# Two interleaved attention layers: normalised rows shared with GpSimd, more PSUM places, a new order, fewer waits

## The chip, the core and the metric

The kernel runs on one core of a Trainium2 chip. A core has five engines with queues of their own: TensorE (PE, matmuls into PSUM), VectorE (DVE), ScalarE (ACT), GpSimd (POOL) and SyncE (SP, which issues transfers). PSUM, into which TensorE writes, has eight banks of 512 f32 per partition. The metric is the device time of one execution in microseconds; lower is better.

## The reference

Two blocks, A and B, are each applied twice to x of 2048 rows and 512 columns, 32 heads of 16:

```
x = x + A(layernorm(x)); x = x + B(layernorm(x))      # twice

A: for each of 4 segments of 512 rows:
   a_dot = softmax(q k^T * scale + causal mask) v
   a_mem = phi(q) M / (phi(q) z + 1e-6)               # phi(t) = t+1 if t > 0 else exp(t)
   o = g * a_mem + (1 - g) * a_dot
   M += phi(k)^T v;  z += sum(phi(k))
B: phi_q = [softmax(q w), softmax(-q w)], phi_k alike  # per head
   o = phi_q (phi_k^T v) / (phi_q sum(phi_k) + 1e-6)
each followed by a product with wo
```

## The kernel before

The program first builds a list of 3416 operations (`Program.add`), each with its engine or a choice of engines, its inputs and outputs as tiles, and a planner's cost. Nothing is planned when it runs: four tables written out in the file fix everything. `ORDER` lists the operations in the order in which the queues are filled; a number of 10000 and more is a score operation whose matmuls are interleaved with those of the one before it, and a negative number is a group of idle matmuls on a tile of zeros (L1431), which keep TensorE's clock up. `ENGINE` has one letter for each operation that has a choice of engines. `SLOTS` has a digit for each tile: which buffer, or which PSUM place of its kind, it gets. `AFTER` is a list of 126 pairs (x, y). `replay` reads the tables, and `finalize` turns each operation's needs into semaphore waits.

A pair (x, y) of `AFTER` makes operation x wait for operation y, though y is no input of x (`ops[x].need.add(y)` at the end of `replay`). In all 126 x stands on GpSimd and y on VectorE.

The rows are handled in tiles of 128. For each segment of 512 rows and each layer, the work is:

- `ln` (L790 on): per row tile the statistics (`stats`, L801; `aggr`, L802), the reciprocal deviation (`veps` and `pow`, L811 and L813, mostly on GpSimd; L807 and L808 on ScalarE), and the normalised rows `xn` (L817, VectorE, two tiles a buffer). A transposing transfer from SP's queue then makes xnT (tiles xA, xB or EQ) of them; at the start and at the turn between the layers TensorE transposes instead (L601).
- `a_proj`: q, k and v for block A; the copies out of PSUM (`k.copy`, `q.copy`, `v.copy`, all by the helper at L579) are on ScalarE or VectorE by `ENGINE`; small rearrangements `lo` (L907) and `kp` (L938) on VectorE, ScalarE or GpSimd; `phik`, `phiq` on ScalarE and VectorE.
- `a_att`: 288 score operations (`score`, 36 for each segment and layer), each filling a pair of PSUM banks, each followed by one exponential of 128 x 1024 on ScalarE (`exp`, L1104, into a tile PT). On the diagonal tiles follow two masks: `mask.odd` (L1110, tile D, VectorE or GpSimd) and `mask.even` (L1113, in place in PT, GpSimd). Then the products with v (`pv`), their division (`r1` and `norm`, L1138 and L1139), the memory's part (`amadd`, L1149), the output product and the addition to X (L1165; or through TensorE with `resid.act` at L579).
- `b_keys`, `b_queries`, `b_out`: block B, whose exponentials are at L1200 and L1285, sums at L1207 (GpSimd) and L1209, `bk.z` at L1220 to L1222 (ScalarE, VectorE or GpSimd), `bq.wide` at L1304 (ScalarE or GpSimd), divisions at L1342.

All matmuls but the idle ones and the transposes have line L520. The kinds of PSUM places are in `self.PS.kinds`: "st" a pair of banks for a score operation; "gen" and "pv" one bank for a single result; "two" and "wide" are those of block B's output and of the turn and the tail.

Blocks A and B, and the segments, are woven into each other by `ORDER`. Each engine works its queue strictly in that order.

Of the kernel before, what the change touches and what calls it, by code (L numbers as in the profile page):

```python
# [275 lines left out]
class Program:  # L276
# [22 lines left out]
    def R(self, *key):  # L299
        r = self.fixed.get(key)  # L300
        if r is None:
            r = self.fixed[key] = Res()
        return r
# [49 lines left out]
    def replay(self):  # L353
# [34 lines left out]
        for x, y in AFTER:  # L388
            ops[x].need.add(y)
# [1086 lines left out]
```

## Time and profile before

| | |
|---|---|
| median of 3 runs | 478.36 us (478.14 to 478.48) |
| the profiled execution | 478.63 us, of which its span 476.9 us |
| granted TensorE clock | 1.00 over the span |
| transfers | 35.86 MB in 115091 packets, mean 75 GB/s |

A group in the profile reads: line, engine, operation, out<-in by tile names, shapes, count | busy us, mean ns of one | idle time of the engine before them, and what ended most of it. A wait reads: who waited <- for whom: total us, times, longest. A row of the time line reads: start, length, engine, line, operation. PE is TensorE's matmuls, PEld its weight loads, which run ahead beside them. Times in rows are us from the span's start.

The kernel has a lead-in of some 13 us (loads, first statistics), two layers of four segments, a turn between the layers near 200 to 240 us, and a tail from about 440 us.

### The profile page before, as it was taken

The numbers are of one execution on the slowest core, as the hardware profiler recorded it, in microseconds if no ns is written. First come the engines' busy times: TensorE is split into PE (matmuls) and PEld (weight loads), VectorE is DVE, ScalarE is ACT, GpSimd is POOL, SyncE is SP. The second block draws the span as 40 slices with busy tenths as digits, with TensorE's granted clock in tenths as the row PEclk, the third lists the DMA queues.
The fourth block names the chain that finished last, engine by engine and source line by source line (L and its number), as shares of the span: only waits on it lengthen the run. The fifth ranks groups of instructions, "written<-read, shape, count | busy, mean of one in ns | idle before, by whom it ended". The sixth has DMA issues, their size and how long they took to land.

```text
span 476.9 us, 19206 instructions
## 1 busy us (share of the span) xinstructions
PE 465.2 (98%) x8309; PEld 319.3 (67%) x8309; DVE 424.0 (89%) x1008; ACT 429.7 (90%) x666; POOL 268.9 (56%) x435
## 2 busy tenths in 40 slices
PE   7999999999999999999999999999999999999997
PEld 6786677567756567557687666766765666665763
DVE  6999899989998988688999999999998888978885
ACT  3989999999999999986799899989999999999742
POOL 3686758656756685510267575784677578761100
DMA  8679661342422132320346417155434121313366
GB/s 264 115 202 147 144 92 25 69 69 47 48 46 47 25 65 51 36 55 4 67 62 97 74 21 134 25 75 83 59 63 63 25 47 33 51 38 58 70 128 186
DMA packets 115091, 35.86 MB, mean 75 GB/s; under 512 B 106816, under 2 KB 115008, under 8 KB 115008
## 3 DMA queue, kind: packets, MB, share of 16 engines
q1 hardware_dynamic: 112608, 32.54, 38.3%
q10 hardware_dynamic: 2400, 2.11, 1.4%
q8 instruction: 65, 1.06, 0.9%
q14 instruction: 18, 0.15, 0.1%
HBM read 6.32 MB, written 2.10 MB: 18 GB/s over the span
## 4 chain that ended last, share of the span: by engine, by line
PE 59%; DVE 18%; ACT 17%; DMA 3%; POOL 2%; issue 1%; POOLq 0%; DVEq 0%
PE PS L520 57%; ACT PT L1104 12%; DVE D L1110 2%; DVE stats L801 2%; DVE Vt L1228 2%; ACT Ek L1200 2%; DVE xn L817 1%; PE PS L601 1%; DMA EQ<-xn 1%; PE PS L1431 1%; DMA OT<-O 1%; DVE O L1139 1%; ACT K L1285 1%; DVE X L1165 1%; DVE Zk L1209 1%
## 5 line engine op out<-in xcount | busy, mean ns | idle before, releaser
L1104 ACT ACTIVATE PT<-PS 128x1024 bf16<-128x1024 f32 x288 | 284.6, 1083 | 7.8 <-PE PS L520 7.5
L1110 POOL TENSOR_TENSOR D<-PT,modd 128x256 bf16<-128x256 bf16 x133 | 91.6, 699 | 54.2 <-ACT PT L1104 39.1
L1113 POOL TENSOR_SCALAR_AFFINE_SELECT PT<-PT 128x512 bf16<-128x512 bf16 x128 | 83.9, 664 | 30.8 <-DVE D L1110 27.4
L520 PEld LDWEIGHTS PS<-VT,PT 128*128 128x128 bf16 x2048 | 75.0, 96 | 19.2 <-POOL PT L1113 2.5
L520 PE MATMUL PS<-VT,PT 128*128 128x17 bf16 x2048 | 82.4, 171 | 0.7 <-POOL PT L1113 0.2
L520 PE MATMUL PS<-QT,K 32*128 32x64 bf16 (+2 forms) x2176 | 77.9, 213 | 0.3
L520 PE MATMUL PS<-VT,D 128*128 128x17 bf16 x512 | 59.9, 170 | 0.0
L520 PEld LDWEIGHTS PS<-QT,K 32*128 32x128 bf16 x2176 | 41.5, 93 | 20.6 <-ACT PT L1104 10.5
L1110 DVE TENSOR_TENSOR D<-PT,modd 128x256 bf16<-128x256 bf16 x123 | 42.9, 362 | 2.9 <-ACT PT L1104 1.5
L520 PEld LDWEIGHTS PS<-VT,D 128*128 128x128 bf16 x512 | 43.2, 96 | 0.0
L1228 DVE TENSOR_TENSOR Vt<-PS,Zk 128x1024 bf16<-128x1024 f32 (+1 forms) x34 | 39.0, 1158 | 2.0 <-PE PS L520 1.0
L801 DVE BATCH_NORM_STATS2 stats<-X 128x6 f32<-128x512 bf16 x56 | 37.3, 681 | 2.5 <-DMA X<-in_A_x_dram 2.2
L1200 ACT ACTIVATE Ek<-PS 128x512 bf16<-128x512 f32 x64 | 37.6, 664 | 0.9 <-PE PS L520 0.9
L520 PE MATMUL PS<-WA_v,xA 128*128 128x256 bf16 x256 | 36.6, 273 | 0.1
L520 PE MATMUL PS<-WA_k,xA 128*128 128x256 bf16 x256 | 36.3, 273 | 0.2 <-POOL xA L907 0.2
L520 PE MATMUL PS<-xA,WA_q 128*128 128x128 bf16 x512 | 35.7, 219 | 0.5 <-DVE MS L986 0.2
L1165 DVE TENSOR_TENSOR X<-X,PS 128x512 bf16<-128x512 bf16 x50 | 33.7, 679 | 2.2 <-PE PS L520 1.8
L1207 POOL TENSOR_TENSOR Vt<-Ek 128x512 f32<-128x512 bf16 x24 | 27.9, 1164 | 12.9 <-ACT Ek L1200 10.4
L520 PEld LDWEIGHTS PS<-xA,WA_q 128*128 128x128 bf16 x512 | 29.8, 98 | 4.6 <-issue 0.6
L520 PE MATMUL PS<-WA_o,OT 128*128 128x512 bf16 x128 | 32.0, 380 | 0.6 <-DMA OT<-O 0.4
L520 PE MATMUL PS<-WB_o,OT 128*128 128x512 bf16 x128 | 32.1, 379 | 0.1
L1304 POOL COPY O<-rho 128x512 bf16<-128x512 bf16 x24 | 14.9, 634 | 26.5 <-DVE rho L1297 23.3
(157 smaller groups left out, 980.7 us busy)
## 6 DMA issues: line engine op xcount, KB each, us to landing
X<-in_A_x_dram SPq DMA_DIRECT2D x3, 512.0 KB, 9.9
EQ<-in_B_wqkv_dram SPq DMA_DIRECT2D x2, 512.0 KB, 5.4
out_dram<-X SPq DMA_DIRECT2D x8, 128.0 KB, 2.0
out_dram<-X ACTq DMA_DIRECT2D x8, 128.0 KB, 1.9
OT<-O SPq DMA_TRANSPOSE x42, 3.2
WB_v<-in_B_wqkv_dram SPq DMA_DIRECT2D x1, 512.0 KB, 4.3
WA_o<-in_A_wo_dram SPq DMA_DIRECT2D x1, 512.0 KB, 6.5
WB_o<-in_B_wo_dram SPq DMA_DIRECT2D x1, 512.0 KB, 4.7
```

The source lines that it names most:

```text
L520: return e.matmul(o, l, r, start=st, stop=sp, tile_position=(basep(l), basep(o)))
L601: ins = e.transpose(self.bank(gen).bitcast(BF16)[:, dt * 128:(dt + 1) * 128], src()[:, dt * 128:(dt + 1) * 128], self.ident[:])
L801: self.dve(lambda e, t=t, src=src: e.bn_stats(self.stats[:, t, :], src()), 0.603, [held() if held else R("X", t)], [R("stats", t)], name=" ...
L817: self.dve(lambda e, t=t, n=n, xn=xn: e.tensor_scalar(xn.ap[:, n], self.X[:, t, :], self.mv[:, t, 0:1], self.rstd[:, t:t + 1], op0=ALU.sub ...
L1104: self.act(lambda e, st=st, pt=pt: e.activation(pt.ap[:].rearrange("p b c -> p (b c)"), self.ps[:, st.slot[0] * 512:st.slot[0] * 512 + 102 ...
L1110: self.either(lambda e, d=d, k=k, pt=pt: e.tensor_tensor(d.ap[:, :, k, :].rearrange("p b (z c) -> p b z c", z=2), self.ends(pt.ap[:, :, 25 ...
L1113: self.pool(lambda e, q=quarters: e.affine_select(q(), q(), [[0, 4], [1, 128]], ALU.is_ge, 0.0, base=0, channel_multiplier=-1), 0.6, [pt() ...
L1165: self.dve(lambda e: e.tensor_tensor(X[:, t, :], X[:, t, :], self.bank(gen), ALU.add), 0.6, [R("X", t), gen()], [R("X", t)], name="resid")
L1200: self.act(lambda e, sgn=sgn, Ek=Ek, gen=gen: e.activation(Ek.ap[:, sgn, :], self.bank(gen), ACT.Exp, scale=1.0 - 2.0 * sgn), 512, [gen()] ...
L1207: self.pool(lambda e, Ek=Ek, sums=sums: e.tensor_tensor(sums(), *(Ek.ap[:].rearrange("p s (h j) -> p s h j", h=H)[:, :, :, 8 * k:8 * k + 8 ...
L1228: self.dve(lambda e, w=w, n=n, Vt=Vt, Zk=Zk, gen2=gen2: e.tensor_tensor(self.signed(Vt)[:, w, :, 0:16], self.bank(gen2).rearrange("p (h d) ...
L1304: P.add(("act", "pool"), {"act": lambda e, dst=dst, src=src: e.activation(dst(), src(), ACT.Copy), "pool": lambda e, dst=dst, src=src: e.t ...
```

## The change

Four things are changed at once.

1. In `ln` the operation `xn` may be on VectorE or on GpSimd (`either` in place of `dve`), the same instruction on either. The new `ENGINE` puts 27 of 64 on GpSimd, 11 in the first layer and 16 in the second.
2. "st" gets the pair of banks 6 and 7; "gen" gets banks 3 and 2.
3. `AFTER` and the two lines of `replay` that read it go: 126 waits of GpSimd for VectorE.
4. `ORDER`, `ENGINE` and `SLOTS` are new. The operations are the same 3416. Idle matmuls are 143 in place of 129, and 75 score operations are interleaved with the one before in place of 67. Of the operations with a choice of engines these change sides (before, then after):

| operation | ScalarE | VectorE | GpSimd |
|---|---|---|---|
| xn | - | 64, 37 | 0, 27 |
| k.copy | 18, 13 | 10, 15 | - |
| v.copy | 17, 16 | 15, 16 | - |
| bk.z | 4, 9 | 7, 6 | 21, 17 |
| bq.wide | 8, 6 | - | 24, 26 |
| resid.act | 12, 10 | 2, 4 | - |
| xnT.copy | 6, 4 | 6, 8 | - |
| boT.copy | 5, 6 | 3, 2 | - |
| fold.copy | 1, 2 | 7, 6 | - |
| kp | 2, 3 | 13, 15 | 17, 14 |
| lo | 6, 6 | 11, 10 | 15, 16 |
| mask.odd | - | 123, 126 | 133, 130 |

```diff
 ORDER = (
...
-AFTER = (
-    (389, 128), (164, 47), (181, 51), (353, 38), (371, 144), (201, 191), (212, 152), (202, 192), (213, 175), (1142, 370), (260, 43), (261, 154),
...
 ENGINE = (
...
 SLOTS = (
...
                 last.mate = op
                 last.need.update(op.need)
             last = op
-        for x, y in AFTER:
-            ops[x].need.add(y)
...
         self.PS.kinds = {
-            "st": [(0, 1), (2, 3), (4, 5)],
+            "st": [(0, 1), (2, 3), (4, 5), (6, 7)],
             "pv": [(7,), (6,), (5,), (4,)],
-            "gen": [(7,), (6,), (5,), (4,)],
+            "gen": [(7,), (6,), (5,), (4,), (3,), (2,)],
             "two": [(6, 7), (4, 5), (0, 1), (2, 3)],
...
             for n, t in enumerate(4 * c + i for i in grp):
-                self.dve(lambda e, t=t, n=n, xn=xn: e.tensor_scalar(xn.ap[:, n], self.X[:, t, :], self.mv[:, t, 0:1], self.rstd[:, t:t + 1],
-                                                                    op0=ALU.subtract, op1=ALU.mult), 0.324,
-                         [R("X", t), R("mv", t), R("rstd", t)], [xn(n)], port=True, name="xn")
+                self.either(lambda e, t=t, n=n, xn=xn: e.tensor_scalar(xn.ap[:, n], self.X[:, t, :], self.mv[:, t, 0:1], self.rstd[:, t:t + 1],
+                                                                       op0=ALU.subtract, op1=ALU.mult), 0.324, 0.63,
+                            [R("X", t), R("mv", t), R("rstd", t)], [xn(n)], name="xn")
```

The numbers 0.324 and 0.63 are the planner's costs and don't reach the chip.

More of the change, by code (lines that the diff above doesn't have):

```diff
@@ L33 @@
 ORDER = (
[137 rows of a table removed]
-)
-AFTER = (
[12 rows of a table removed]
[137 rows of a table added]
 )
 ENGINE = (
-    "daddaadadaadadapaapapadaadaapppddppddpdpdpddpdpdpppppdppddpdpapadpadadpdpdapapaddaddddddppppapapppdppdpdddddppdpdddpdppppdddpppddpddadpaadad"
-    "daaddadddpdapdpppappdpdddddpppdpppdddddddppdpddddppddpddpapaapadaadaddapdpdddpppppppdppddppdddddddddddppdppddddddpddpdpppddadappdpappadaaaaa"
-    "aaaaaadaaapdapdadpaddddddpadaapppppdpdddppddddpdppppdpdppdpddpdadddpdpadaaaadpapadpdppapppddppppppddddpppdddppppppdppddpppppdddapaapaaaapddd"
-    "apapaadpappppppdddddddppdpddpddddppppdppppddddpppdddddddaddaadpaddapddadppppppdpdppppddddpdppdddpdpppddddddpdpppddpddaddpdaapapaasasassasaaa"
-    "aassdads"
+    "dddaddddaaddpdapadapaapddaaaadaadpdpppdpddddddddpdpdppppddppppdpppddpadadpapadpdaddpapaadadddddadddppappapppddpppdpppdppddddddddddppppppdddd"
@@ new lines @@
+    "pppddpdppdddaaadddddpaaddddadpdppapppppppdpppddpdppddpdpddpdddppdddddpdppdddpdpppapaadadaapadddpddaddddddadppppppddpddpppddddddpdddppdpppddd"
+    "dppdpdppdddadddddapddpapppaddaaaadpadadddddaaapaapdaaaaddddaddddaadddpdpppdpdddddddpppppddddppddppdpppdaaddpddadpapadaapddpddpadppapapdppppp"
+    "ppddddpppdddpddpdpdpppdppppddddpdpaapaapapaaddpaaadpdadpdppppappppppdpdpddppdddddddddpddpppdppdppdpdddpppppddddddpdddddadpdddddpddpdaapppppd"
+    "pppppppddpdppddddpdpdppddddppdddddpddadppdddpaappapaasaasssassassasadaaa"
@@ L192 @@
 )
 SLOTS = (
-    "00001102030001020030111201203100120141131150261033007081111329031012001000001131231051221312013312002300037180012120111134021610039001002130"
-    "01301102006021210004019120120031231700001313001120208101100011002711900231111104062201100210203305170010310221130013100381901022313032110310"
-    "00611111004022202331120212233150810310330312020700210328190100113105100210013320710109030231118000012015013000221710100121300113410112503711"
-    "02000131800100202110123003261901201312103415013100021170111220023360211232800913010031310120022170009111051038001011000309011223100037021110"
@@ L198 @@
-    "22025081100302001137190111100003031516031002020021201320040381113112001322130351200161012220133000112323319012303101107120221121214003518000"
-    "10230209031200102001061030271013120411100301052193686272072110202112210012430006121012023333123245167302013210120314500040153201305112300161"
-    "07025123011123210110311001214710050002241011500023203160311110128091001200030710032235022110111124061003011313230028101022101139100021224102"
-    "71001123061101231210021002901113034081031200110310410160212311013017081021010121011000235061213031090101220213000001210310303041002001332210"
@@ L202 @@
-    "35061121322700110238100324130190101001120122210103303001104120171001121001121309100131011030002103204110022117081111200300012011229110020103"
-    "24100300611112280030029131000110212101050710122026101119001310003211713221801112142021035012133222718033119101021314002231112017100503081090"
-    "01113270302024013210518011011000210406110321110700102313203103212109041210320601110001703123213100230301519022112330122218033061123210123506"
-    "13210239011020070113182300001002214130200311501611200122321031023711110008954301673041113200050231103211074036521000721210010314300013412512"
@@ L206 @@
-    "1130101130043156211207122130021306451"
+    "00100102034050000001111220011304100213115061207021030101458092510210102103001023105121112200133413001210819300231031002121060112030137102110"
+    "00213020040233106003107120300041520328000411010022005119000114021708211330104261110200221010230042135370115403103101201200381901230123200103"
+    "10401211126102002311021210233519012133003071020231003081900010021031050213201170110381023021309113110110170100201801132103205111100003113023"
+    "26010401518310040353432030709352302011120304036111103308110122011002122003270110233115091122312073480501330341001010051220801217210900113011"
@@ new lines @@
+    "02102304103025121080911030013341521307320305320433202035250631113011002102113120030271203311101042159240010312400082530100212232150103061201"
+    "01320204091300102301170000228103201051021104126379201121180211030412252502430110030252412330323241506172010223110024534005011670046512172300"
+    "11057221102602214032115030243400103213518020131306073063201110273901504000350381120002111340110023100602333103321221712020910113022105301032"
+    "28112103206132011001103390202421550720100415000100220152205601101117280532001411022050030425014150921021010405010023230610201032101415230134"
@@ new lines @@
+    "15000221133370200812022333111090111201011211006032023321003110017120310100619013111010110030000221300310012021270810100031201200390120421510"
+    "03260130211011035002318101122203413020709130112201050200301110140100923120812000136072120024235110222310432140524829015010223046251100301427"
+    "01022261801102110131171902001210102131021001003380310112202405103600111100113200100302801202024130210023212017160321131251903340601321320207"
+    "10132200600121801303200642930243045200111320040121073035200431250832211069232210140451210250021432211040573031206300401321102216203000227311"
@@ L207 @@
+    "1023622020320041115330211152617405162"
 )
```

285 rows, old and new, of tables (AFTER, ORDER) are left out of this document.

## The prediction

> **What bounds the kernel now.** I read the page first, then the chain, then the stages.
>
> ```profile
> span 476.9 us, 19206 instructions
> PE 465.2 (98%) x8309; PEld 319.3 (67%) x8309; DVE 424.0 (89%) x1008; ACT 429.7 (90%) x666; POOL 268.9 (56%) x435
> PE 59%; DVE 18%; ACT 17%; DMA 3%; POOL 2%; issue 1%; POOLq 0%; DVEq 0%
> PE PS L520 57%; ACT PT L1104 12%; DVE D L1110 2%; DVE stats L801 2%; DVE Vt L1228 2%; ACT Ek L1200 2%; DVE xn L817 1%; PE PS L601 1%; DMA EQ<-xn 1%; PE PS L1431 1%; DMA OT<-O 1%; DVE O L1139 1%; ACT K L1285 1%; DVE X L1165 1%; DVE Zk L1209 1%
> ```
>
> Three engines are busy for nine tenths of the span and the chain runs over all three; GpSimd alone has room, and is on the chain for 2%. The stages (columns: stretch, then busy us of PE, PEld, DVE, ACT, POOL with counts, granted clock, DMA share, GB/s):
>
> ```profile
> 40.00:60.00 20.00, 19.69 (x364) 12.98 (x361) 18.58 (x52) 19.97 (x28) 13.27 (x22) 1.00 0.85 137
> 160.00:180.00 20.00, 19.79 (x370) 12.02 (x369) 18.14 (x45) 19.97 (x31) 15.57 (x24) 1.00 0.21 42
> 200.00:220.00 20.00, 19.41 (x210) 11.71 (x208) 18.07 (x34) 17.02 (x41) 2.96 (x6) 1.00 0.33 41
> 300.00:320.00 20.00, 19.75 (x366) 13.48 (x364) 19.76 (x45) 19.29 (x27) 16.45 (x26) 1.00 0.33 49
> 340.00:360.00 20.00, 19.82 (x473) 14.74 (x473) 18.81 (x53) 20.00 (x26) 12.78 (x21) 1.00 0.47 69
> 440.00:460.00 20.00, 19.52 (x227) 14.58 (x226) 17.11 (x31) 13.45 (x44) 1.62 (x3) 1.00 0.49 95
> ```
>
> In the attention stages (40 to 60, 160 to 180, 340 to 360) ScalarE has no gap left; at 300 to 320 VectorE is the fuller one. At the turn between the layers (200 to 220) and in the tail (440 on) nobody is full and latency rules. A busy PE is not a PE at its peak, so I look at what it waits for:
>
> ```profile
> PEld PS L520 <- ACT PT L1104: 22.0, 68, 0.6
> PEld PS L520 <- issue: 14.5, 62, 0.4
> POOL D L1110 <- ACT PT L1104: 39.1, 32, 3.9
> DVE Zk L1209 <- POOL Vt L1207: 3.8, 4, 1.3
> ```
>
> TensorE's largest wait is for ScalarE's exponentials (22.0 us in 68 pieces). VectorE's largest wait for GpSimd is only 3.8 us. So time is to be won first by taking work from ScalarE, next from VectorE; GpSimd's extra work costs only where it comes in others' way.
>
> **The change part by part.** I laid the letters of ENGINE against the operations in the order in which the program adds them, before and after. That counts what each engine gets; it gives no time.
>
> ScalarE: 12 operations leave it (5 k.copy, 1 v.copy, 2 bq.wide, 2 resid.act, 2 xnT.copy) and 8 come (5 bk.z, 1 kp, 1 fold.copy, 1 boT.copy).
>
> ```profile
> 55.44 0.49 ACT ktok L579
> L579 ACT ACTIVATE ktok<-PS 128x512 bf16<-128x512 f32 x18 | 11.8, 654 | 0.3 <-PE PS L520 0.3
> L1220 ACT ACTIVATE Vt<-Zk 128x64 bf16<-128x64 f32 x4 | 2.0, 511 | 0.0
> ```
>
> In a full queue a 512-wide copy takes 0.49 of the chain, though it lasts 654 ns, since neighbours overlap. So 12 x 0.49 = 5.9 leave; 3 x 0.49 + 5 x 0.38 (0.49 x 511/654) = 3.4 come: **-2.5 us on ScalarE**. I count all of it as time, for ScalarE is full where most of these operations stand.
>
> VectorE: 27 rows leave; 5 k.copy, 2 resid.act, 1 v.copy, 2 xnT.copy, 2 kp and 3 mask.odd come; bk.z, lo, boT.copy and fold.copy lose one each.
>
> ```profile
> L817 DVE TENSOR_SCALAR xn<-X,mv,rstd 128x512 bf16<-128x512 bf16 x64 | 26.3, 427 | 3.5 <-ACT rstd L808 2.3 <-POOL rstd L813 0.6
> L579 DVE CAST ktok<-PS 128x512 bf16<-128x512 f32 x10 | 6.7, 674 | 0.1
> L1110 DVE TENSOR_TENSOR D<-PT,modd 128x256 bf16<-128x256 bf16 x123 | 42.9, 362 | 2.9 <-ACT PT L1104 1.5
> L579 DVE COPY xA<-PS 128x512 bf16<-128x512 bf16 x3 | 1.3, 417 | 0.3 <-PE PS L601 0.3
> ```
>
> -27 x 0.427 = -11.5; 8 casts x 0.674 = +5.4; 2 x 0.417 = +0.8; 3 x 0.362 = +1.1; the other moves (two kp in, four single ones out) lie between 0.3 and 0.7 each and make -1.2: **-5.4 us on VectorE**. It sets the end for 18% of the span, so I take 0.18 x 5.4 = -1.0.
>
> GpSimd: 27 rows come. No row of before shows this operation on GpSimd; the nearest are one-input operations of 512 bf16 elements, and above them a two-input one:
>
> ```profile
> L1304 POOL COPY O<-rho 128x512 bf16<-128x512 bf16 x24 | 14.9, 634 | 26.5 <-DVE rho L1297 23.3
> L1113 POOL TENSOR_SCALAR_AFFINE_SELECT PT<-PT 128x512 bf16<-128x512 bf16 x128 | 83.9, 664 | 30.8 <-DVE D L1110 27.4
> L1110 POOL TENSOR_TENSOR D<-PT,modd 128x256 bf16<-128x256 bf16 x133 | 91.6, 699 | 54.2 <-ACT PT L1104 39.1
> L1207 POOL TENSOR_TENSOR Vt<-Ek 128x512 f32<-128x512 bf16 x24 | 27.9, 1164 | 12.9 <-ACT Ek L1200 10.4
> ```
>
> Between 0.63 and 1.16; I take 0.65, for it has one tensor input: 17.6 us, and the other moves (4 bk.z, 3 kp and 3 mask.odd away, 2 bq.wide and 1 lo more) take about 4 off, **+13 us**, to some 282 of 477. The cover is its idle time. But the row is made 0.65 - 0.43 = 0.22 later, and 1% of the chain is xn L817 (about 5 us, 11 of 64 rows): 27/64 x 11 x 0.22 = +1.0 at most, 0 at least; I take +0.6.
>
> The trn2 pages give a price too: the Trainium skill, "GPSIMD Engine Reference", section 3.1, has 512 elements in a tight loop at about 769 ns; by that estimate the rows would be 20.8 us in place of 17.6, and no run here shows which.
>
> The port: GpSimd and VectorE hold each other up.
>
> ```profile
> 261.80 0.64 POOL L1113 TENSOR_SCALAR_AFFINE_SELECT PT<-PT 128x512 bf16<-128x512 bf16 x1
> 261.81 0.76 DVE L949 TENSOR_SCALAR PhiK<-ktok 128x512 bf16<-128x512 bf16 x1 [0.23 <-PE PS L520]
> 103.47 0.29 DVE L949 TENSOR_SCALAR PhiK<-ktok 128x512 bf16<-128x512 bf16 x1
> 91.56 0.67 POOL L1110 TENSOR_TENSOR D<-PT,modd 128x256 bf16<-128x256 bf16 x1 [0.96 <-DVE X L1165]
> 91.41 0.28 DVE L1110 TENSOR_TENSOR D<-PT,modd 128x256 bf16<-128x256 bf16 x1
> ```
>
> The same VectorE operation takes 0.29 alone and 0.76 when a GpSimd operation began 0.01 us earlier: it ends with GpSimd's. The last two rows show a removed wait at work: GpSimd stood 0.96 us for a residual that is none of its inputs, VectorE's mask took the port at 91.41, and GpSimd came behind it. Of VectorE's masks D, 123 x (0.362 - 0.28) = 10 us are such stalls now. 5% more GpSimd time (13 of 269) makes at most 1 us more over all kinds, 0.18 of it on the chain: +0.2.
>
> The removed waits: 126 pairs, each a GpSimd operation behind a VectorE one that is no input of it. Most are met when GpSimd comes; those that show in the waits view:
>
> ```profile
> POOL D L1110 <- DVE QT L579: 4.0, 1, 4.0
> POOL D L1110 <- DVE xA L907: 3.4, 4, 2.5
> POOL rstd L811 <- DVE r L1138: 2.7, 1, 2.7
> POOL D L1110 <- DVE X L1165: 1.0, 1, 1.0
> ```
>
> With the smaller rows about 15 cases. Without the wait GpSimd may take the port first and VectorE stands for up to 0.66: 15 x 0.66 = 10 us of VectorE, 0.18 of it 1.8; at least 0, or a gain where GpSimd's result was late (3.8 us in the Zk row). I take half, +0.9.
>
> The Trainium skill, "SBUF — State Buffer", section "Who interferes with whom", says that whoever issues first holds the shared pair for the whole instruction and the other blocks; the 0.76 row agrees. By that rule alone, with nothing to order the two, each of the 27 rows can block VectorE for a full 0.65; that is the third rival below, worked out there from rows.
>
> PSUM and order: score pairs stand on banks 0-1, 2-3, 4-5, 6-7 in 132, 97, 33, 26 cases (before 132, 137, 19, none), and 68 of 289 single results go to banks 2 and 3. It is the same eight banks, so no room is added, only choice. Paired score operations rise from 67 to 75, idle matmuls from 129 to 143.
>
> ```profile
> 64.83 0.58 PE L1431 MATMUL PS<-warm 128*128 128x240 bf16 x4
> 100.88 0.39 PE L520 MATMUL PS<-QT,K 32*128 32x256 bf16 x4
> ```
>
> 14 idle matmuls at about 0.1 are +1.4 us where the order expects TensorE to wait anyway; 8 more pairs save up to 0.2 each, -1.6: together 0. The order itself could win part of the 22.0 us or lose as much; I enter 0 and keep both ends.
>
> Sum: -2.5 - 1.0 + 0.6 + 0.2 + 0.9 = **-1.8 us**. The profiled execution took 478.63 with its span of 476.9, 0.27 over the median 478.36 of the runs; so 476.8 for it and **476.5** for the median.
>
> **The rivals.**
> 1. The new order with its free choice of banks shortens TensorE's many small waits. For it: 22.0 us in 68 pieces, none over 0.6, and full ScalarE. Against: the same eight banks, and most pairs still on four of them. A third of the 22 us: 476.5 - 7 = 469.5; I give it 471.
> 2. The change doesn't reach the end: VectorE's relief falls into its own slack, and the moved copies only trade places. 478.4, within 0.2%.
> 3. The port makes VectorE the bound (slower). 27 x 0.65 = 17.6 us of GpSimd rows and 10 us behind the removed waits stand in VectorE's way, less 5.4 relief: +22 us on VectorE. It decides where VectorE is over 19 of 20 us, as at 300 to 320; at 0.18 to 0.4 of the chain this is +4 to +9, so 482.5 to 487; I take 483.
>
> **How the numbers follow.** Forecast 0.36 (474 to 477.3), rival 1 0.18, rival 2 0.17, rival 3 0.29. Forecast 476.5. The range takes most of rival 1 and the lower half of rival 3: 470 to 483.5. About 0.2%, 1 us, is what a measurement of this kernel can tell from no change. Faster 0.54, same 0.17, slower 0.29.
>
> **What would show it.** xn rows on GpSimd near 0.65 us (near 1.16 refutes the price); ScalarE busy lower by 2 to 3 us and VectorE by about 5; the D mask's mean on VectorE at 0.36 to 0.39: over 0.42 means rival 3. Rival 1 shows as a PEld wait for PT L1104 well under 22 us. I am wrong if VectorE's busy time rises although 27 operations left it, or if the turn between the layers, 200 to 240, or the tail grows by over 2 us.

## The result and the profile after

| | before | after |
|---|---|---|
| median of 3 runs | 478.36 us (478.14 to 478.48) | 510.42 us (503.38 to 511.63) |
| profiled execution, its span | 478.63, 476.9 us | 511.63, 509.9 us |
| granted TensorE clock in the profiled execution | 1.00 | 0.96 |

By the medians the change makes the kernel 32 us slower. The ratio after to before is 1.0591, its 95% interval 1.0463 to 1.0719, which is some 28 us: it leaves out the run of 511.63 us, which counts as a slow one, being over 1.5% above the shortest run of its kernel. The three runs of after had granted clocks of 0.960, 0.963 and 0.983, and the lower the clock the longer the run; the profiled execution is the longest of them. The same long rows, waits and dips of the clock are seen in e2 below.

The page of after: span, busy time, granted clock by slice, the chain by engine and by line, then two groups.

```profile
span 509.9 us, 19163 instructions
PE 472.7 (93%) x8260; PEld 327.0 (64%) x8323; DVE 427.9 (84%) x992; ACT 430.3 (84%) x662; POOL 322.0 (63%) x455
PEclk9989979899999999999997999979998999979999
PE 41%; DVE 19%; ACT 18%; POOL 12%; DMA 6%; issue 4%; POOLq 0%; DVEq 0%
PE PS L504 38%; ACT PT L1088 13%; POOL xn L801 4%; POOL D L1094 3%; POOL PT L1097 3%; DVE D L1094 3%; DMA EQ<-xn 3%; ACT Ek L1184 2%; DVE AM L993 2%; DVE stats L785 2%; DVE X L1149 2%; PE PS L1415 2%; POOL rstd L797 1%; DVE Vt L1212 1%; DVE xn L801 1%
L1088 ACT ACTIVATE PT<-PS 128x1024 bf16<-128x1024 f32 x288 | 284.0, 1062 | 28.5 <-PE PS L504 27.6
L801 POOL TENSOR_SCALAR xn<-X,mv,rstd 128x512 bf16<-128x512 bf16 x27 | 57.8, 2140 | 15.9 <-ACT rstd L792 14.5
```

Line numbers have moved by 16 (the exponential L1104 is now L1088, the masks L1110 and L1113 are L1094 and L1097). ScalarE is busy for the same time as before (430.3 against 429.7 us), and the exponentials last no longer (284.0 against 284.6). What is new is below the totals. A row on GpSimd takes **2.14 us**, not 0.65. GpSimd's share of the chain is 12% where it was 2%, and the top item of it is xn. The clock row has dips to 0.7 where before had none.

The waits of after (who waited <- for whom: total us, times, longest):

```profile
ACT PT L1088 <- PE PS L504: 27.6, 40, 2.4
PEld PS L504 <- ACT PT L1088: 20.1, 57, 1.4
DVE r L1122 <- PE PS L504: 16.4, 21, 3.4
PE PS L504 <- POOL PT L1097: 6.3, 9, 1.7
PE PS L504 <- DMA EQ<-xn: 2.9, 4, 1.0
```

ScalarE, which had hardly a gap, now waits 27.6 us for TensorE's scores; in before the rows for the same waits read:

```profile
ACT PT L1104 <- PE PS L520: 7.5, 17, 1.1
PE PS L520 <- POOL PT L1113: 0.2, 1, 0.2
PE PS L520 <- DMA EQ<-xn: 0.2, 1, 0.2
```

TensorE's own wait for the exponentials has not grown (22.0, now 20.1 us). What has grown are its waits for the mask PT on GpSimd, from 0.2 to 6.3 us, and for the transfers that transpose the normalised rows, from 0.2 to 2.9 us for EQ alone. Stretches of after (stretch, then busy us of PE, PEld, DVE, ACT, POOL, granted clock, DMA share, GB/s):

```profile
40.00:60.00 20.00, 18.64 (x326) 12.41 (x327) 18.01 (x43) 19.49 (x29) 16.62 (x23) 1.00 0.72 107
60.00:80.00 20.00, 17.11 (x325) 12.56 (x324) 16.15 (x41) 16.28 (x24) 16.19 (x21) 0.83 0.56 82
80.00:100.00 20.00, 17.51 (x333) 12.22 (x334) 16.67 (x38) 16.51 (x22) 14.21 (x22) 0.83 0.28 41
320.00:340.00 20.00, 18.09 (x280) 11.78 (x271) 18.63 (x42) 15.11 (x20) 17.63 (x25) 0.83 0.14 28
```

and two of the same stretches before:

```profile
60.00:80.00 20.00, 19.46 (x435) 15.25 (x433) 18.98 (x48) 19.49 (x28) 13.36 (x24) 1.00 0.45 66
80.00:100.00 20.00, 19.13 (x367) 13.31 (x367) 19.56 (x46) 19.12 (x26) 13.44 (x21) 1.00 0.37 61
```

The loss is not spread evenly. From 40 to 60 the stage is nearly as full as it was; from 60 to 100 every engine but GpSimd loses between 1.1 and 3.2 us in each 20, and the clock falls too. (The same times hold not quite the same work in the two kernels.) The chain of after through such a stretch (start, length, what):

```profile
258.67 1.29 POOL D L1094 x2
259.96 0.23 POOL rstd L795
260.19 0.67 POOL D L1094
260.86 0.68 POOL rstd L797
261.54 0.60 POOL PT L1097
...
262.35 1.54 POOL PT L1097 x2
263.89 2.06 POOL xn L801
265.96 0.60 POOL PT L1097
266.56 2.09 POOL xn L801
268.65 0.68 POOL D L1094
...
269.45 1.33 POOL PT L1097 x2
270.78 0.41 POOL xA L891
...
271.24 10.15 PE PS L504 x172
```

For 12 us the chain runs over GpSimd and hardly anything else. Its queue is served in order, so the masks D and PT and the small copy xA stand behind two rows of 2.06 and 2.09 us; only when they are done does TensorE get its 10 us of matmuls.

**The theories.** (T1) The price of the row on GpSimd is the loss, through GpSimd's queue. (T2) The removed waits are: GpSimd takes the port and VectorE stands. (T3) The new order and banks are worse by themselves. (T4) The fall of the clock makes a small delay large.

### The profile page after: what moved, and what is told of

It reads as the page before. It is cut to its first block, busy times and chain, and to the rows that moved or that the text cites. A ratio compares the mean times of both kernels' runs of the same rounds, so it can differ in the third digit from the quotient of the medians.

```text
span 509.9 us, 19163 instructions
## 1 busy us (share of the span) xinstructions
PE 472.7 (93%) x8260; PEld 327.0 (64%) x8323; DVE 427.9 (84%) x992; ACT 430.3 (84%) x662; POOL 322.0 (63%) x455
## 4 chain that ended last, share of the span: by engine, by line
PE 41%; DVE 19%; ACT 18%; POOL 12%; DMA 6%; issue 4%; POOLq 0%; DVEq 0%
PE PS L504 38%; ACT PT L1088 13%; POOL xn L801 4%; POOL D L1094 3%; POOL PT L1097 3%; DVE D L1094 3%; DMA EQ<-xn 3%; ACT Ek L1184 2%; DVE AM L993 2%; DVE stats L785 2%; DVE X L1149 2%; PE PS L1415 2%; POOL rstd L797 1%; DVE Vt L1212 1%; DVE xn L801 1%
## 5 line engine op out<-in xcount | busy, mean ns | idle before, releaser
L1088 ACT ACTIVATE PT<-PS 128x1024 bf16<-128x1024 f32 x288 | 284.0, 1062 | 28.5 <-PE PS L504 27.6
L1094 POOL TENSOR_TENSOR D<-PT,modd 128x256 bf16<-128x256 bf16 x130 | 88.7, 693 | 31.7 <-ACT PT L1088 31.0
L1097 POOL TENSOR_SCALAR_AFFINE_SELECT PT<-PT 128x512 bf16<-128x512 bf16 x128 | 83.9, 664 | 30.5 <-DVE D L1094 28.2
L504 PEld LDWEIGHTS PS<-VT,PT 128*128 128x128 bf16 x2048 | 76.2, 97 | 28.5 <-POOL PT L1097 5.7
L801 POOL TENSOR_SCALAR xn<-X,mv,rstd 128x512 bf16<-128x512 bf16 x27 | 57.8, 2140 | 15.9 <-ACT rstd L792 14.5
L504 PEld LDWEIGHTS PS<-QT,K 32*128 32x128 bf16 x2176 | 41.1, 94 | 24.0 <-ACT PT L1088 10.2
L1094 DVE TENSOR_TENSOR D<-PT,modd 128x256 bf16<-128x256 bf16 x126 | 43.8, 365 | 5.7 <-PE PS L504 3.0
L504 PE MATMUL PS<-WA_k,xA 128*128 128x256 bf16 x256 | 38.7, 285 | 2.6 <-POOL xA L891 2.0
L504 PE MATMUL PS<-WA_v,xA 128*128 128x256 bf16 x256 | 39.3, 285 | 1.4 <-DMA xA<-xn 0.7
L504 PE MATMUL PS<-xA,WA_q 128*128 128x128 bf16 x512 | 37.5, 226 | 1.2 <-DMA xA<-xn 0.6
L504 PEld LDWEIGHTS PS<-xA,WA_q 128*128 128x128 bf16 x512 | 31.6, 101 | 5.2 <-issue 1.4
L1122 DVE RECIPROCAL r<-PS 128x16 f32<-128x16 f32 (+1 forms) x72 | 16.7, 235 | 16.6 <-PE PS L504 16.4
```

Of the source, the lines that this page charges most:

```text
L504: return e.matmul(o, l, r, start=st, stop=sp, tile_position=(basep(l), basep(o)))
L801: self.either(lambda e, t=t, n=n, xn=xn: e.tensor_scalar(xn.ap[:, n], self.X[:, t, :], self.mv[:, t, 0:1], self.rstd[:, t:t + 1], op0=ALU. ...
L1088: self.act(lambda e, st=st, pt=pt: e.activation(pt.ap[:].rearrange("p b c -> p (b c)"), self.ps[:, st.slot[0] * 512:st.slot[0] * 512 + 102 ...
L1094: self.either(lambda e, d=d, k=k, pt=pt: e.tensor_tensor(d.ap[:, :, k, :].rearrange("p b (z c) -> p b z c", z=2), self.ends(pt.ap[:, :, 25 ...
L1097: self.pool(lambda e, q=quarters: e.affine_select(q(), q(), [[0, 4], [1, 128]], ALU.is_ge, 0.0, base=0, channel_multiplier=-1), 0.6, [pt() ...
L1122: self.dve(lambda e, r1=r1, view=view, nt=nt: e.reciprocal(r1.ap[:, 0:nt, :], view()[:, :, :, 16]), 0.07 + 0.0475 * nt, [pv()], [r1()], na ...
```

## The experiments

Each ratio is to before, timed on the same chip beside it.

**e1: the rows back on VectorE, all else as after.**

```diff
+            if op.name == "xn":
+                op.on = "dve"
```

> The changed kernel (its order, its banks, no removed waits put back) with all 64 normalised rows on VectorE, at the same places of the order. Theory price (a GpSimd row takes 2.1 us, not 0.65, and all else follows from it): 474 to 482 us, granted clock 1.00, ScalarE's wait for PE at L1088 back from 27.6 us to under 12. Rival order (the new order and banks are themselves worse): above 492. Rival waits (the 126 removed waits were needed): above 485, with the D mask on VectorE over 0.40 us in the mean.

490.22 us, ratio 1.0237 (1.0213 to 1.0261). The time missed the 474 to 482 that T1 alone would give, and ScalarE's wait for TensorE came back to 13.1 us, not under 12. It is under the 492 of the rival order; it is above the 485 of the rival waits, but the D mask on VectorE has a mean of 0.353 us, not over 0.40. Busy times of the run:

```profile
PE 466.4 (96%) x8323; PEld 320.1 (66%) x8323; DVE 433.3 (89%) x1019; ACT 429.1 (88%) x662; POOL 267.1 (55%) x428
```

20 of the 32 us are gone, with the clock back at 0.996. The 12 us that remain over before are not explained by this run: the waits are gone too (e3), and the other moves had loaded VectorE in exchange for the rows, so that with the rows back it carries 433.3 us, 9.3 more than before.

**e2: before, with the same 27 rows on GpSimd; its order, banks and 126 waits kept.**

```diff
+XN = (341, 342, 462, 751, ...)
...
+            if op.name == "xn":
+                op.on = "pool" if op.i in XN else "dve"
...
```

> The kernel before, with nothing changed but that the same 27 rows go to GpSimd, its 126 waits and its order kept. Theory price: rows at about 2.1 us, GpSimd busy up by 27 x 2.1 = 57 us, time 495 to 520, clock under 1.00. Rival order: under 485, for the loss then comes with the order.

509.06 us, ratio 1.0628 (1.0604 to 1.0652), clock 0.966 in the profiled execution.

```profile
PE 477.8 (94%) x8309; PEld 324.9 (64%) x8309; DVE 420.1 (83%) x981; ACT 432.5 (85%) x666; POOL 327.4 (64%) x462
L822 POOL TENSOR_SCALAR xn<-X,mv,rstd 128x512 bf16<-128x512 bf16 x27 | 59.8, 2216 | 14.0 <-ACT rstd L813 12.9 <-DMA xA<-xn 0.2
```

The rows alone, in the old order and with the waits, make the whole loss. ScalarE's wait for TensorE is 24.6 us here. That is T1; T3 isn't needed for it, and neither is T2.

**e3: before, without the 126 waits and nothing else.**

```diff
-        for x, y in AFTER:
-            ops[x].need.add(y)
```

> The kernel before without the 126 waits, all else kept. Theory price: 476 to 480. Rival waits: above 485. My prediction's own term for it was +0.9 us (0 to 1.8).

482.56 us, ratio 1.0093 (1.0072 to 1.0114), clock 1.00: between the two expectations.

```profile
PE 465.7 (97%) x8309; PEld 319.3 (66%) x8309; DVE 428.1 (89%) x1008; ACT 430.7 (90%) x666; POOL 270.0 (56%) x435
PE 47%; DVE 29%; ACT 18%; DMA 3%; issue 1%; POOL 1%; DVEq 0%
```

VectorE is busy 4.1 us longer (428.1 against 424.0), its share of the chain goes from 18% to 29%, and the time rises by 4.2 us over the 478.33 of its before. T2 is real, but about an eighth of the 32 us.

**e4, e5, e6: after, with a cheaper operation in the 27 GpSimd rows.** Order, banks, engines and waits are after's; only what GpSimd does in the row is varied (in short):

```diff
-  pool: tensor_scalar(xn, X, mv, rstd, op0=subtract, op1=mult)
+  e4:   tensor_scalar(xn, X, 0.0, 20.0, op0=subtract, op1=mult)
+  e6:   tensor_scalar(xn, X, rstd, None, op0=mult)
+  e5:   tensor_copy(xn, X)
```

> The changed kernel, but its 27 GpSimd rows subtract and multiply by two constants in place of the row's mean and deviation, so that part of the normalisation is left out; they wait for the same inputs. If the two per-partition scalars make the price: rows at 0.6 to 0.8 us and the time that the prediction meant, 474 to 480. If the two-step arithmetic makes it: rows still at about 2.1 us and the time 500 to 513.

> The changed kernel, but its 27 GpSimd rows are plain copies of x (the normalisation of those rows is left out); they wait for the same inputs. This gives the rows the price that I assumed, about 0.61 us (row of the copies at L1304). If the rows' price is the one large error and the removed waits cost 4 us as in the run with the waits alone, 474 to 482 us at clock 1.00. If the order and the banks are bad in themselves, above 490.

> The changed kernel, but its 27 GpSimd rows only multiply by the deviation (one step, one per-partition scalar; the mean is left out). If the second arithmetic step makes the price: rows at 0.6 to 0.9 us and 474 to 484 us. If any TENSOR_SCALAR on GpSimd is slow: rows at 1.0 to 1.9 us and 488 to 503.

The group of the rows in each, e5 first, then e6, then e4 (count | busy us, mean ns of one | idle before):

```profile
L802 POOL COPY xn<-X 128x512 bf16<-128x512 bf16 x27 | 17.1, 635 | 14.3 <-ACT rstd L792 13.4
```

```profile
L802 POOL TENSOR_SCALAR xn<-X,rstd 128x512 bf16<-128x512 bf16 x27 | 43.7, 1617 | 14.7 <-ACT rstd L792 13.3
```

```profile
L802 POOL TENSOR_SCALAR xn<-X 128x512 bf16<-128x512 bf16 x27 | 52.9, 1960 | 16.6 <-ACT rstd L792 14.4
```

| run | us of one row | time, us | ratio to before | ScalarE's wait for TensorE, us | clock |
|---|---|---|---|---|---|
| e5, copy | 0.635 | 481.14 | 1.0057 (1.0031 to 1.0083) | 9.1 | 1.000 |
| e6, one step with a scalar per partition | 1.617 | 496.15 | 1.0377 (1.0338 to 1.0415) | 17.9 | 0.990 |
| e4, two steps with constants | 1.960 | 505.79 | 1.0565 (1.0534 to 1.0597) | 24.7 | 0.983 |
| after, two steps with scalars per partition | 2.140 | 510.42 | 1.0591 (1.0463 to 1.0719) | 27.6 | 0.960 |

All three fell in the branch in which the row's length sets the time: rows of 1.6 us and more came with over 488 us, the copy with 474 to 482. This is the deciding series: one order, one set of engines, and the time follows the length of the row. From first to last 29.3 us of time by the medians, some 26 by the ratios, stand against 27 x (2.140 - 0.635) = 40.6 us of GpSimd time, 0.6 to 0.7 a microsecond. e5 is the kernel that the prediction had reckoned with, row of 0.635 us and all. It takes 481.14, 2.1 over its before of 479.01. The page of e5:

```profile
PE 463.8 (97%) x8323; PEld 319.4 (67%) x8323; DVE 425.5 (89%) x992; ACT 427.6 (89%) x662; POOL 281.4 (59%) x455
PE 43%; ACT 27%; DVE 20%; DMA 5%; POOL 2%; issue 2%; SPq 0%; POOLq 0%; DVEq 0%
```

GpSimd is back to 2% of the chain, and its 281.4 us are the 282 that the prediction's sum gave.

**e7: after's order, banks and missing waits, with every operation on the engine that it had before.**

```diff
-ENGINE = (after's letters)
+ENGINE = (before's letters)   # and the 64 rows on VectorE
```

> The changed kernel's order, banks and lack of waits, with every choice of engine as before (rows on VectorE, copies as before). If the run with the rows back is slow because VectorE then has 6 us more work than before, this gives the 4 us back or more: 480 to 486, near the kernel before without its waits (482.6). If the order and banks are bad by themselves, it stays at 488 or above.

496.83 us, ratio 1.0376 (1.0352 to 1.0401); VectorE 435.9 us busy, ScalarE 433.1. The expectation of 480 to 486 failed, and by its other branch (488 or above) order and banks are bad by themselves. With the old sides they are: 17.8 us over before, 13.6 more than the waits alone cost in e3. With the sides that they came with they are not, for e5 has the same order and banks and is 2.1 over before. That an order fixed for one set of engines is a poor one for another would explain both; no run shows it by itself.

**e8: e2 with the 11 rows of the first layer only.**

```diff
-XN = (27 rows)
+XN = (the 11 of the first layer)
```

> The kernel before with only the 11 first-layer rows of the 27 on GpSimd. If each slow row costs about the same, 11/27 of the 30.7 us: 489 to 493. If only a few late rows matter, or the clock's fall needs many, it lies off that line: under 486 or over 496.

493.65 us, ratio 1.0315 (1.0279 to 1.0352): 14.6 us for 11 rows, 1.33 each, against 30.7 / 27 = 1.14 each in e2. That is just above the 489 to 493 of the first branch. The loss grows about with the number of rows, slightly less than in proportion; so the rows of the second layer alone don't make it, and eleven rows on GpSimd would not have been free. Which rows of a layer cost most was not tried.

**e9: before without its 129 groups of idle matmuls. e10: after with each group of idle matmuls twice.** They ask about T4.

```diff
 e9     if x < 0:
+           continue
 e10        self.queues["pe"].append(f.i)
+           g = self.idle_op((-1 - x) // 16, (-1 - x) % 16)
+           g.done = n
+           self.queues["pe"].append(g.i)
```

> The kernel before without the 129 idle matmuls that ORDER asks for (the six of the start stay); nothing else changes. It asks what a lower granted clock costs by itself, in an order whose engines are otherwise not disturbed: the idle matmuls stand where TensorE would wait, 20.3 us in all, so without them TensorE has less to do, not more. If the clock's fall is a large part of the loss of the changed kernel, the clock falls here to about 0.96 and the time rises to 490 or more with every other engine's busy time as before. If the clock is only a sign of the waits and costs little, the time stays within 478 to 483 even where the clock falls. I expect the second, about 482 at a clock of 0.98.

> The changed kernel with each of its 143 groups of idle matmuls given twice; the GpSimd rows stay at 2.1 us. If the fall of the clock to 0.96 is what turns the late rows into so much time, the second helping holds the clock nearer to 1 and the time falls by 5 us or more, to 505 or less. If the late rows cost through their waits alone, the doubled matmuls lie in TensorE's waits or add up to 23 us of work, and the time stays at 508 to 516 with the clock little changed. I expect the second.

e9: 485.54 us, ratio 1.0156 (1.0118 to 1.0193), between the two expectations. The busy times of VectorE and GpSimd hardly move (422.7 and 268.4 us against 424.0 and 268.9). The clock falls in three of the stretches of 20 us, to 0.91 in two of them and furthest here, where every engine does less:

```profile
160.00:180.00 20.00, 18.04 (x348) 10.68 (x347) 16.68 (x42) 18.64 (x28) 12.72 (x21) 0.83 0.30 29
```

before had 19.97 of ScalarE and clock 1.00 there. (1 - clock) x span is the clock time that is lost: in e9's four runs 6.8, 10.2, 12.2 and 8.7 us, on average 9.5, for 6.7 us of time. If all of the 6.7 is the clock's, a microsecond of lost clock costs about 0.7 in this kernel. Runs of one kernel with different clocks give a similar figure: in after 18.8 us lost at a span of 508.7 and 8.5 at 501.7, which is 7.0 / 10.3 = 0.68; between the longest and the shortest run it is 0.5 in e2 and 0.8 in e10. Such runs may differ in more than the clock, so this is an estimate.

The Trainium skill, "TensorE: Matmul & The Clock Gate", section "Terms", takes the penalty to be the throttled time times (1 - K/N), which, read as time of the kernel, is a whole microsecond for each one lost. By that the 9.5 would have cost 9.5; the 6.7 measured is less. TensorE has 50% of e9's chain, so that a slower TensorE need not be felt everywhere; that this is the reason is not shown.

e10: 513.15 us, ratio 1.0712 (1.0663 to 1.0762). Against its expectation the clock did rise, to between 0.980 and 0.993 in its four runs; the time did not fall. Its chain:

```profile
PE PS L507 48%; ACT PT L1091 6%; PE PS L1418 6%; POOL xn L804 5%; DVE D L1097 2%; POOL PT L1100 2%; DVE Vt L1215 2%; POOL D L1097 2%; DVE stats L788 1%; DVE X L1152 1%; POOL rstd L800 1%; DVE Zk L1196 1%; DVE O L1126 1%; DMA xA<-xn 1%; DMA EQ<-xn 1%
```

The idle matmuls (here L1418) are now 6% of the chain, where after had 2%. They held the clock higher, and what that won was not seen in the time; the work that they add is the likely reason. So e10 shows that this remedy is none, not that the clock costs nothing.

**What is settled and what is not.** The length of the row is the cause (e2; e5, e6, e4 in one order), and the waits add 4 us (e3). How much of the 32 us passes through the clock is an estimate: after's median run lost (1 - 0.963) x 508.7 = 18.8 us of clock, at 0.5 to 0.8 some 9 to 15 us, and the rest would be waits as such. No run here takes the clock's fall out of after without adding work. The new order and the new banks were not priced apart from each other, and the waits were not tried on the new order. No version tried was faster than before.

## Why the prediction was wrong, point by point

- **What bounds the kernel**: right as a reading of before. Wrong in what was drawn from it, "GpSimd's extra work costs only where it comes in others' way": it came in others' way often, for the masks stand in the same queue and TensorE's products with v wait for them (0.2 us of waits for the mask PT before, 6.3 after; GpSimd's share of the chain 2%, then 12%).
- **GpSimd, 27 rows of 0.65 us**: this is the step that failed. The row is 2.140 us; the term of 17.6 us was 57.8. It was priced by counting tensor inputs, and the upper bound of 1.16, a two-input operation, was no bound: the two-step operation with one input lasted 2.140 us, longer than that two-input one of one step. The 13 us for GpSimd are right apart from that: it got 53.1 more, of which 57.8 - 17.6 = 40.2 are this error. The Trainium skill's price of the prediction, "GPSIMD Engine Reference", section 3.1 (20.8 us), came out nearly as low: its 769 ns for 512 elements is near the copy (635), not near this operation (2140). Where no row of before shows an operation on an engine, the range has to say so: 483.5 held nothing of it.
- **The later row, +0.6 us**: the wait for the row was priced by the 1% of the chain that xn had. This failed too, apart from the row's length: with the measured row the same term gives 27/64 x 11 x (2.140 - 0.427) = 7.9 us at most, where after lies some 26 to 29 us over e5. A longer row also delays what stands behind it on its engine, and that was not in the sum at all.
- **Removed waits, +0.9 us**: mis-sized, 4.2 measured, and over its bound of 1.8. The cases were about as priced (half of 10 us is 5, VectorE's busy time rose by 4.1); the factor 0.18 was wrong. VectorE's share of the chain before did not price added VectorE time: it became 29%, and the kernel took 4.2 us longer for 4.1 us more of VectorE.
- **ScalarE, -2.5 us**: e5 has 427.6 against 429.7, -2.1. The count of moves was right. That it turned into time is not shown.
- **VectorE, -5.4 us**: it became +3.9 in after and +1.5 in e5. Of the 9.3 us between forecast and after, the waits explain 4.1, if e3 carries over. The forecast also took the full lengths of the operations, though neighbours overlap on VectorE as on ScalarE (by 0.08 us in rows shown below); for 16 operations fewer that is some 1.3 us too much. The rest fits operations that got longer beside GpSimd: the first PhiK operation 412 ns against 352, the first PhiQ one 418 against 374, KP 375 against 319. The prediction's own sign of error, VectorE rising although 27 operations left it, came true.
- **The port, +0.2 us, and rival 3**: the time lay beyond rival 3's, but not for its reason. The D mask's mean on VectorE is 365 ns against 362 and 0.42 was the point at which rival 3 was to be believed. The mask alone was too narrow a sign, for PhiK, PhiQ and KP did get longer. But from e5 to after, with rows over three times as long, VectorE's busy time grew by only 2.4 us (425.5, then 427.9) and the time by over 25, so the port is a small part. What GpSimd's rows held up was above all GpSimd's own queue, and then the transfers of the rows themselves.
- **PSUM, order and idle matmuls, 0**: open. With the row as assumed, e5 is 2.1 over before; if e3's 4.2 carries over, the rest of the change is worth about -2, near the prediction's -2.7 without the waits. So even at the assumed price the sign would have been wrong (1.0057, interval 1.0031 to 1.0083), by this reckoning through the waits.
- **Rival 1** fell with its test row: 20.1 us, not well under 22.

## What to carry to other kernels

A move to an idle engine is priced by a row of that very operation on that engine, and where there is none, by measuring it before anything else; operations with the same tensor input differed here by a factor of over three (0.635 to 2.140 us). What it then costs is read from what stands behind it in that engine's queue and who waits for that, not from the engine's idle share. The share of the chain that an engine has is a share at one balance: in e3 time added to an engine that was busy for 89% of the span was paid for in full (4.1 us of VectorE, 4.2 us of the kernel).

## What the hardware showed that was not expected

**One tensor input does not tell GpSimd's price.** On 128x512 bf16, one input each: copy 0.635 us, one step with a scalar per partition 1.617, two steps with constants 1.960, two steps with scalars per partition 2.140. The largest jump, 0.98 us, is from the copy to any TENSOR_SCALAR; the second step adds 0.52, scalars per partition in place of constants 0.18. One step with a constant was not tried.

**A long GpSimd operation doesn't keep VectorE out for its whole length.** Three rows of after on GpSimd (start, length, engine, line, operation):

```profile
40.45 2.07 POOL L801 TENSOR_SCALAR xn<-X,mv,rstd 128x512 bf16<-128x512 bf16 x1
...
133.75 2.22 POOL L801 TENSOR_SCALAR xn<-X,mv,rstd 128x512 bf16<-128x512 bf16 x1
...
263.88 2.08 POOL L801 TENSOR_SCALAR xn<-X,mv,rstd 128x512 bf16<-128x512 bf16 x1
```

and VectorE beside them:

```profile
42.02 0.65 DVE L944 TENSOR_SCALAR PhiQ<-QT 128x512 bf16<-128x512 bf16 x1
...
134.61 0.28 DVE L944 TENSOR_SCALAR PhiQ<-QT 128x512 bf16<-128x512 bf16 x1
134.81 0.29 DVE L1094 TENSOR_TENSOR D<-PT,modd 128x256 bf16<-128x256 bf16 x1
...
264.02 0.76 DVE L944 TENSOR_SCALAR PhiQ<-QT 128x512 bf16<-128x512 bf16 x1
```

The same PhiQ took 0.76 us when it began 0.14 after the row, and 0.28 when it began 0.86 after it, with over 1 us of the row still to go; the mask behind it took its usual 0.29. The Trainium skill, "SBUF — State Buffer", section "Who interferes with whom", has the first comer hold the shared pair for the whole instruction. A hold agrees with the 0.76, but for the whole instruction it does not agree with the 0.28 and 0.29. The held PhiQ ended 0.90 us after the row began (264.02 + 0.76 - 263.88); as it takes 0.28 unheld, it was let go some 0.6 us after the row began. Nor is the row's end free: the PhiQ at 42.02 began 1.57 us after its row, took 0.65 and ended 0.15 after the row. Among the other rows of after it is the same: VectorE's xn, PhiQ and PhiK that began 0.14 to 0.42 us after a row ended 0.90 to 0.96 after it, PhiQ and PhiK that began 0.65 to 1.48 after it took 0.27 to 0.29, and PhiQ, PhiK, KP and xn that began 1.57 to 1.77 after it ended 0.14 to 0.15 after the row's end, while single D masks that began then took their 0.28. So these rows hold VectorE up at their start and at their end, and not between; this fits rows over three times as long adding only 2.4 us to VectorE.

**The clock fell where TensorE waited in small pieces.** TensorE was busy for 17.1 of 20 us between 60 and 80 in after, its longest wait for another engine there was 1.4 us, and the clock was 0.83; at 18.6 of 20 between 40 and 60 it was 1.00. The busy share of a stretch doesn't decide it alone: in e9 the clock was 0.83 at 18.04 of 20 (160 to 180) and 1.00 at 17.76 (440 to 460). What decides it was not tested.
